# Later batches' squares of q and k: accumulated unfolded by DMA instead of folded on VectorE and then accumulated

## The chip, the cores and the metric

The kernel runs on 1 core of one Trainium2 chip. Its metric is the device time in microseconds (us) of one execution; lower is better. A profile of one execution goes with it, and its times are counted from the start of the profiled span.

## The reference

q, k and v are 4 x 6080 x 256 (batch, rows, columns) in fp32. Cut to what matters:

```
qn = q / (norm(q, over the 6080 rows) + 1e-6)
kn = k / (norm(k, over the 6080 rows) + 1e-6)
a  = softmax(kn^T @ qn / tau)              # 256 x 256 for each batch
x  = (v @ a) as 24320 tokens of 256
h  = relu(x @ w_in)                        # 256 -> 2048
out = (s * h*h + b) @ w_out                # 2048 -> 256
```

The norms are what the change is about: for each batch and each of the 256 columns of q and of k, the sum of 6080 squares.

## The kernel before, in words

**Two kinds of work share the core.** The token part goes through 48 groups of up to 512 tokens, each in 16 steps (`FT`). A step m of group g does the first product (`mm1`, L641: two matmuls into `h_ps`, which has two buffers), seven or eight small matmuls of the second product for the group before (L809), every second step a Relu from PSUM on ScalarE (L651), and squares and sums of the hidden values on VectorE and ScalarE (L662, L664, L735 to L741). VectorE also takes the results out of PSUM (L669). Each group stores 512 KB through the SP queue (L676) and transposes the next v tiles with four DMA transposes on the same queue (L401).

**The attention part runs ahead by one batch.** Batch 0's attention is computed at the start. For b = 1, 2, 3 its pieces are laid between the token steps of batch b - 1 by hand: `at_step(s, f)` puts f after the matmuls of step s, and `po` keeps every engine's instructions in the order in which they are written. A later batch has 12 chunks (`chunks_later`): eleven of 128 partitions with 4 rows each (`JC` = 4), and one of 112. The start step of chunk c is `sc = w0 + span * c * JC / n`; chunks are some 6.75 steps apart in batch 1 and 9.75 in batches 2 and 3. For each chunk:

- `load` (L130): k and q to fp16 by two casting DMAs on the POOL queue, 16 steps ahead of `sc`, into `qk_pool` (8 buffers);
- `mm` (L146): the Gram products of k and q, accumulated in PSUM over the batch;
- `norm_ops`: the squares and what becomes of them, one operation every three steps from `sc` + 3.

**`norm_ops` before the change.** The squares of k (ScalarE, L169) and of q (VectorE, L166) go to a tile `sq` of 128 x 2 x 4 x 256 fp16 in `sq_pool`, which has two buffers for each tag. Two `fold`s on VectorE (L182) add its four rows to two and then to one, giving a tile of 128 x 2 x 1 x 256 (128 KB) in `f3_pool`. Of a later batch, chunk 0's and the last chunk's folded tile are kept in `self.rows`; those of the ten chunks between are added onto chunk 0's by a DMA on the POOL queue (`into_first`, L193):

```
dst, src = self.rows[0][0][0][:np_], st["f", 1][:np_]
po(nc.gpsimd.dma_start(out=dst, in_=src, accum_op=ALU.add))
```

**The end of a batch.** `finish_ops` starts 54 steps ahead of the next batch's first group. Its first operation, `add_norms` (L224), sums the tiles in `self.rows` over the partitions with one-column matmuls; roots, reciprocals, the scaling, the exponentials and the folding of `a` into w_in follow.

**The POOL queue** issues in its written order the loads of k and q, the loads of v (L379, into 4 buffers) and the accumulating DMAs; an instruction that waits holds those behind it.

Of the kernel before, what the change touches and what calls it, by code (L numbers as in the profile page):

```python
# [9 lines left out]
FP16 = mybir.dt.float16  # L10
FP32 = mybir.dt.float32
AF = mybir.ActivationFunctionType
ALU = mybir.AluOpType
# [3 lines left out]
def kernel(  # L17
# [12 lines left out]
    nc = tc.nc  # L30
    P = 128

    B, N, C = q.shape
# [20 lines left out]
    def po(ins):  # L54

        tc.keep_in_program_order(ins)
        return ins

    def pool(name, bufs, **kw):
        return ctx.enter_context(tc.tile_pool(name=name, bufs=bufs, **kw))  # L60
# [3 lines left out]
    wpool = pool("wpool", 1)  # L64
    qk_pool = pool("qk_pool", 8)
    sq_pool = pool("sq_pool", 2)
    f3_pool = pool("f3_pool", 13)
    sm_pool = pool("sm", 1)
    apool = pool("apool", 2)
# [22 lines left out]
    JC = 4  # L92
# [16 lines left out]
    class Gram:  # L109
# [45 lines left out]
        def norm_ops(self, c):  # L155

            qc, kc = self.tiles[c]
            _, np_, jc = self.chunks[c]
            st = {}

            def squares(a, js):
                def f():
                    if "sq" not in st:
                        st["sq"] = sq_pool.tile([P, 2, JC, C], FP16, tag="sq", name="sq")
                    if a == 0:
                        po(nc.vector.tensor_mul(  # L166
                            st["sq"][:np_, 0, js, :], qc[:np_, js, :], qc[:np_, js, :]))
                    else:
                        po(nc.scalar.activation(  # L169
                            out=st["sq"][:np_, 1, js, :], in_=kc[:np_, js, :], func=AF.Square))  # L170
                return f

            def fold(half, arrays, last):
                def f():
                    src = st["f", 2 * half] if 2 * half < jc else st["sq"]
                    if ("f", half) not in st:
                        if last:
                            t = f3_pool.tile([P, 2, 1, C], FP16, tag="f3", name="f3")
                        else:
                            t = sq_pool.tile([P, 2, half, C], FP16, tag=f"f{half}", name="f")  # L180
                        st["f", half] = t
                    po(nc.vector.tensor_add(  # L182
                        st["f", half][:np_, arrays], src[:np_, arrays, :half, :],
                        src[:np_, arrays, half : 2 * half, :]))
                    if last and (self.b == 0 or c == 0 or c == len(self.chunks) - 1):
                        for rows in self.rows:
                            rows.append((st["f", half], np_, 1))
                return f

            def into_first():  # L190

                dst, src = self.rows[0][0][0][:np_], st["f", 1][:np_]
                po(nc.gpsimd.dma_start(out=dst, in_=src, accum_op=ALU.add))  # L193

            def unfolded():
                for rows in self.rows:
                    rows.append((st["sq"], np_, jc))

            ops = []
            for h in range(0, jc, 4):  # L200
                js = slice(h, min(h + 4, jc))
                ops += [squares(1, js), squares(0, js)]
            if jc == 2:
                return ops + [unfolded]
            if jc == 8:
                ops += [fold(4, slice(0, 1), False), fold(4, slice(1, 2), False)]
            ops += [fold(2, slice(0, 2), False), fold(1, slice(0, 2), True)]
            return ops + [into_first] if self.b > 0 and 0 < c < len(self.chunks) - 1 else ops

        def add_norms(self, arrays=(0, 1), last=False):  # L210

# [258 lines left out]
    for c in range(NCH0 - 2):  # L470
        ops = g0.norm_ops(c)
# [11 lines left out]
    ops = [g0.norm_ops(c) for c in (NCH0 - 2, NCH0 - 1)]  # L483
# [21 lines left out]
    acc = opool.tile([P, 4, C], FP32, tag="o_sb", name="acc")  # L505
# [50 lines left out]
    for i, f in enumerate(fin[12:]):  # L556
        at_step(FOLDS[i], f)
    at_step(14, lambda: po(nc.vector.tensor_scalar_mul(
        out=s_out, in0=s_bc, scalar1=1.0 / (LAM * LAM))))
# [341 lines left out]
```

## Time and profile before

| what | us |
|---|---|
| median of 3 runs | 718.86 |
| lowest and highest run | 718.62, 719.0 |
| the profiled execution: its span | 717.2 (717.15 in the trace) |
| runs' median above that span | 1.7 |
| TensorE busy, share of the span | 698.9, 97% |
| VectorE busy | 626.1, 87% |
| ScalarE busy | 536.5, 75% |
| L182 folds, 94 in all, of these 72 for batches 1 to 3 | 0.685 and 0.420 each |
| L193 accumulating DMAs, 30 of 128 KB | 3.1 from issue to landing (median) |

The profiled execution's own time is read from its span, since the page lists no other time for it; the device times of the runs include what lies around the span. "Busy" is the time in which an engine has an instruction at work. PE is TensorE, PEld its weight loads, DVE VectorE, ACT ScalarE, POOL GpSimd, SP SyncE. The DMA share is the mean busy share of the core's 16 DMA engines, in tenths in the page's slices. The granted TensorE clock is 1.000 throughout.

### The profile page before, as it was taken

The page shows a single profiled execution, that of the slowest core. Times are in us where ns is not written, and L with a number is a line of the kernel's source. Part 1 is how long each engine was busy: PE and PEld are TensorE (multiplying, and loading weights), DVE is VectorE, ACT ScalarE, POOL GpSimd, SP SyncE. Part 2 cuts the span into 40 slices and gives each one's busy share as a digit, 9 for nine tenths or more (in the row PEclk, how much of TensorE's full clock was granted, in tenths as well). Part 3 has the DMA queues.
Part 4 walks back from the last instruction along what each step waited for, and adds up shares of the span by engine and source line. Part 5 has one row for each costly group of instructions (what it writes and reads, how often), then busy time and mean ns, then how long its engine had stood idle before and what let it go on. Part 6 is the DMA issues. An engine that isn't in the chain of part 4 may idle for free.

```text
span 717.2 us, 17629 instructions
## 1 busy us (share of the span) xinstructions
PE 698.9 (97%) x7479; PEld 504.6 (70%) x7479; DVE 626.1 (87%) x882; ACT 536.5 (75%) x579; POOL 109.8 (15%) x189
## 2 busy tenths in 40 slices
PE   4799999999999999999999999999999999999998
PEld 2556777776677777777677777777668777777777
DVE  4879999999789999999889899999887888888886
ACT  4479877787777777777777778777877777777875
POOL 4532332101201222111110222110000000000000
PEclk9999999999999999999999999999999999999999
DMA  9999998647556879443972877944423333321201
GB/s 236 207 259 172 159 170 137 111 108 129 119 107 114 144 133 145 108 93 83 154 151 57 141 138 124 154 90 86 105 63 75 93 71 74 97 60 46 83 30 74
DMA packets 89790, 84.25 MB, mean 117 GB/s; under 512 B 59664, under 2 KB 64848, under 8 KB 89712
## 3 DMA queue, kind: packets, MB, share of 16 engines
q0 software_dynamic: 26064, 43.40, 37.5%
q1 hardware_dynamic: 63072, 38.43, 21.5%
q8 instruction: 58, 0.95, 0.6%
q10 hardware_dynamic: 576, 1.31, 0.5%
q14 instruction: 20, 0.16, 0.1%
HBM read 78.91 MB, written 24.90 MB: 145 GB/s over the span
## 4 chain that ended last, share of the span: by engine, by line
PE 93%; DMA 4%; DVE 1%; ACT 1%; POOL 1%; issue 0%; POOLq 0%; ACTq 0%
PE h_ps L641 45%; PE o_ps L809 40%; PE s_ps L146 4%; DMA qk<-in_q_dram 3%; PE wa_ps L326 2%; DMA v<-in_v_dram 1%; PE o_ps L713 1%; PE o_ps L687 0%; POOL qk L130 0%; ACT r L651 0%; DVE o_sb L669 0%; DVE S L737 0%; DVE sq L166 0%; DVE S L735 0%; DVE S L739 0%
## 5 line engine op out<-in xcount | busy, mean ns | idle before, releaser
L651 ACT ACTIVATE r<-h_ps 128x1024 f16<-128x1024 f32 (+1 forms) x384 | 388.4, 1014 | 153.4 <-PE h_ps L641 150.9
L641 PE MATMUL h_ps<-vT,wa 128*128 128x512 f16 (+7 forms) x1632 | 452.1, 364 | 0.1
L809 PEld LDWEIGHTS <-S 128*128 128x128 f16 x2944 | 198.0, 98 | 85.0 <-issue 0.9
L809 PEld LDWEIGHTS <-g 128*128 128x128 f16 x2208 | 155.0, 98 | 74.1
L664 DVE TENSOR_TENSOR g<-r 128x2048 f16<-128x2048 f16 (+2 forms) x150 | 174.8, 1165 | 14.6 <-ACT r L651 14.5
L809 PE MATMUL o_ps<-T,S 128*128 128x128 f16 x2208 | 183.3, 219 | 0.1
L641 PEld LDWEIGHTS <-wa 128*128 128x128 f16 x1632 | 135.9, 98 | 20.6 <-ACT wa L319 0.3
L809 PE MATMUL o_ps<-w_out,g 128*128 128x128 f16 x1472 | 134.2, 219 | 0.2 <-DVE u L669 0.2
L669 DVE SCALAR_TENSOR_TENSOR o_sb<-o_ps,s_out,u 128x256 f32<-128x256 f32 x138 | 66.5, 482 | 47.1 <-PE o_ps L809 44.5
L662 ACT ACTIVATE g<-r 128x1024 f16<-128x1024 f16 (+1 forms) x97 | 100.4, 1035 | 0.2
L146 PE MATMUL s_ps<-qk 128*128 128x256 f16 (+1 forms) x384 | 69.6, 281 | 14.0 <-ACT qk L137 8.7
L379 POOL DMA_DIRECT2D v<-in_v_dram x48 | 31.3, 656 | 263.5 <-DMA vT<-v 209.6
L669 DVE SCALAR_TENSOR_TENSOR u<-o_ps,s_out,rowconst 128x256 f32<-128x256 f32 x138 | 66.0, 478 | 0.0
L809 PE MATMUL o_ps<-w_out,S 128*128 128x128 f16 x736 | 63.5, 219 | 0.0
L809 PE MATMUL o_ps<-N,g 128*128 128x128 f16 x736 | 63.4, 219 | 0.0
L193 POOL DMA_DIRECT2D f<-f x30 | 26.3, 877 | 225.6 <-DVE f L182 172.0
L169 ACT ACTIVATE sq<-qk 128x1024 f16<-128x1024 f16 (+3 forms) x49 | 50.4, 1033 | 10.0 <-DMA qk<-in_k_dram 6.7
L737 DVE TENSOR_TENSOR S<-S,g 128x2048 f16<-128x2048 f16 (+1 forms) x47 | 56.4, 1201 | 1.3
L735 DVE TENSOR_TENSOR S<-g 128x2048 f16<-128x2048 f16 (+1 forms) x47 | 56.1, 1193 | 0.0
L741 DVE TENSOR_TENSOR S<-g,S 128x2048 f16<-128x2048 f16 x46 | 56.0, 1217 | 0.0
L739 DVE TENSOR_TENSOR S<-g 128x2048 f16<-128x2048 f16 x46 | 55.9, 1216 | 0.0
L146 PEld LDWEIGHTS <-qk 128*128 128x128 f16 (+1 forms) x384 | 32.8, 101 | 20.1 <-DVE qk L136 8.0
(74 smaller groups left out, 314.9 us busy)
## 6 DMA issues: line engine op xcount, KB each, us to landing
out_dram<-o_sb SPq DMA_DIRECT2D x46, 512.0 KB, 3.0
v<-in_v_dram POOLq DMA_DIRECT2D x47, 256.0 KB, 4.7
qk<-in_k_dram POOLq DMA_DIRECT2D x42, 256.0 KB, 6.1
qk<-in_q_dram POOLq DMA_DIRECT2D x42, 256.0 KB, 7.2
f<-f POOLq DMA_DIRECT2D x30, 128.0 KB, 3.1
vT<-v SPq DMA_TRANSPOSE x182, 3.2
w<-in_moe_w_out_dram POOLq DMA_DIRECT2D x4, 512.0 KB, 11.3
raw<-in_k_dram SPq DMA_DIRECT2D x2, 512.0 KB, 6.4
```

The source lines that it names most:

```text
L146: po(nc.tensor.matmul(self.s_ps[:, ch, :], kc[:np_, j, ts(ch, P)], qc[:np_, j, :], start=(c == 0 and j == 0 and ch == 0), stop=(c == len(s ...
L169: po(nc.scalar.activation(out=st["sq"][:np_, 1, js, :], in_=kc[:np_, js, :], func=AF.Square))
L641: po(nc.tensor.matmul(dst, wa[:, ci, ts(m, P)], src, start=(ci == 0), stop=(ci == CH - 1), skip_group_check=True))
L651: po(nc.scalar.activation(out=r16[:, :, i % 2, :n], in_=h_tiles.pop((g, i))[:, :, :n], func=AF.Relu))
L662: po(nc.scalar.activation(out=dst, in_=src, func=AF.Square))
L664: po(nc.vector.tensor_mul(dst, src, src))
L669: po(nc.vector.scalar_tensor_tensor(out=dst, in0=src, scalar=s_out, op0=ALU.mult, in1=add, op1=ALU.add))
L735: po(nc.vector.tensor_add(T[1], A21, A22))
L737: po(nc.vector.tensor_sub(T[2], T[1], A11))
L739: po(nc.vector.tensor_sub(T[3], A11, A21))
L741: po(nc.vector.tensor_sub(T[4], A12, T[2]))
L809: po(nc.tensor.matmul(st[name][:, j, :], a()[:, i, ts(j, P)], w[:, i, :], start=first, stop=last, skip_group_check=True))
```

## The change

The ten middle chunks of each later batch are no longer folded. Chunk 0's squares of such a batch go to a tile `sq` of their own in a new pool `acc_pool` with one buffer. Each middle chunk's `sq` tile is added onto it as it is, 128 x 2048 fp16 (512 KB), by an accumulating DMA on the POOL queue, which is now the third operation of a chunk in place of the fifth. After the last chunk's squares come two folds of the accumulated tile and then the two folds of its own. `fold` takes the tile to fold as an argument. Batch 0 is as it was. On VectorE 60 fold instructions fall away; the instructions of TensorE, ScalarE and SP are the same, in the same order; POOL issues as many DMAs as before.

```
+    acc_pool = pool("acc_pool", 1)
...
+            acc = self.b > 0 and c == 0
+
             def squares(a, js):
                 def f():
                     if "sq" not in st:
-                        st["sq"] = sq_pool.tile([P, 2, JC, C], FP16, tag="sq", name="sq")
+                        st["sq"] = (acc_pool if acc else sq_pool).tile([P, 2, JC, C], FP16, tag="sq", name="sq")
...
-            def fold(half, arrays, last):
+            def fold(half, arrays, last, st=st, np_=np_):
...
-                    if last and (self.b == 0 or c == 0 or c == len(self.chunks) - 1):
+                    if last:
                         for rows in self.rows:
                             rows.append((st["f", half], np_, 1))
...
             def into_first():
 
-                dst, src = self.rows[0][0][0][:np_], st["f", 1][:np_]
-                po(nc.gpsimd.dma_start(out=dst, in_=src, accum_op=ALU.add))
+                po(nc.gpsimd.dma_start(out=self.acc["sq"][:np_], in_=st["sq"][:np_],
+                                       accum_op=ALU.add))
...
-            ops += [fold(2, slice(0, 2), False), fold(1, slice(0, 2), True)]
-            return ops + [into_first] if self.b > 0 and 0 < c < len(self.chunks) - 1 else ops
+            if acc:
+                self.acc = st
+                return ops
+            if self.b > 0 and c < len(self.chunks) - 1:
+                return ops + [into_first]
+            if self.b > 0:
+                ops += [fold(half, slice(0, 2), half == 1, self.acc, P) for half in (2, 1)]
+            return ops + [fold(half, slice(0, 2), half == 1) for half in (2, 1)]
```

## The prediction, made before the changed kernel was run

> **What bounds the kernel now.** I read the page's busy table, chain and slices first.
>
> ```profile
> PE 698.9 (97%) x7479; PEld 504.6 (70%) x7479; DVE 626.1 (87%) x882; ACT 536.5 (75%) x579; POOL 109.8 (15%) x189
> ...
> DMA  9999998647556879443972877944423333321201
> ...
> PE 93%; DMA 4%; DVE 1%; ACT 1%; POOL 1%; issue 0%; POOLq 0%; ACTq 0%
> ```
>
> TensorE sets the end: 93% of the chain. So VectorE time taken away is worth only what TensorE waits for VectorE. DMA is full early and light late, so I cut the span into the stretches where batches 1, 2 and 3 are squared.
>
> ```profile
> core 0: us, PE busy (x) PEld busy (x) DVE busy (x) ACT busy (x) POOL busy (x), PEclk, DMA share, GB/s
> ...
> 66.00:78.00 12.00, 11.70 (x123) 8.34 (x121) 11.61 (x16) 12.00 (x18) 2.13 (x4) 1.00 1.14 205
> 78.00:118.00 40.00, 40.00 (x431) 29.53 (x429) 38.12 (x57) 31.16 (x34) 14.29 (x22) 1.00 1.01 159
> 118.00:144.00 26.00, 26.00 (x281) 18.86 (x279) 25.25 (x38) 19.89 (x21) 4.27 (x6) 1.00 0.66 116
> 212.00:300.00 88.00, 87.99 (x949) 64.24 (x946) 80.70 (x114) 67.97 (x71) 18.80 (x29) 1.00 0.71 128
> 385.00:470.00 85.00, 84.99 (x915) 62.16 (x914) 78.89 (x112) 66.14 (x69) 18.72 (x29) 1.00 0.73 129
> ```
>
> TensorE is idle in one of them alone, 66 to 78 us (0.30 us). VectorE is nearly full in batch 1 (38.12 of 40) but holds nobody. The DMA share is the number to keep: 1.01 in batch 1 (over 1 because packets of two queues overlap on an engine), 0.71 and 0.73 in batches 2 and 3. Next, what the edit touches: the folds and their DMA, from the tile view of f, and one such DMA alone on the engines, in slices.
>
> ```profile
> L182 DVE TENSOR_TENSOR f<-sq x47: 680/685/694, 11.6 to 482.4; 128x1024 f16<-128x1024 f16 x44, 112x1024 f16<-112x1024 f16 x3
> L182 DVE TENSOR_TENSOR f<-f x47: 414/420/426, 12.3 to 484.6; 128x512 f16<-128x512 f16 x44, 112x512 f16<-112x512 f16 x3
> ...
> DMA to landing us min/median/max: 2.7/3.1/6.0
> ```
>
> ```profile
> 241.80:242.00 0.20, 0.20 (x5) 0.17 (x4) 0.20 (x1) 0.20 (x1) 0.00 (x0) 1.00 0.73 113
> 242.00:242.20 0.20, 0.20 (x7) 0.20 (x5) 0.06 (x1) 0.01 (x1) 0.13 (x1) 1.00 1.20 179
> 242.20:242.40 0.20, 0.20 (x5) 0.12 (x3) 0.00 (x0) 0.00 (x0) 0.20 (x1) 1.00 1.13 169
> 242.40:242.60 0.20, 0.20 (x2) 0.10 (x1) 0.18 (x1) 0.00 (x0) 0.20 (x1) 1.00 1.09 164
> 242.60:242.80 0.20, 0.20 (x4) 0.15 (x3) 0.20 (x1) 0.00 (x0) 0.20 (x2) 1.00 0.30 31
> ```
>
> The 128 KB accumulate issued at 240.40 moves data from 241.8 to 242.7: about 0.89 us of all 16 engines, at some 170 GB/s, and lands 2.7 us after issue.
>
> **What the Trainium skill says.** All four places are in "DMA: Bandwidth & Descriptors". "Anatomy of one DMA — SWDGE (gpsimd) path" prices a GpSimd DMA at about 2.0 us + bytes/436e3: estimated 2.3 us for 128 KB, 3.2 us for 512 KB. The trace has 2.7 alone and 3.1 median for the first; none shows the second. "SDMA does more than copy" says that the accumulating unit takes at most 2048 elements; a row of the new transfer is exactly 2 x 4 x 256 = 2048, so I count one piece per row; no run shows it yet. "Issuing engines are not separate DMA queues" says that transfers from all issuing engines share 16 DMA engines; the 1.01 and the landing spread of 2.7 to 6.0 agree. "Rules for kernel authors" says that an accumulate reads its destination before it writes it, and that an earlier DMA's semaphore on the same bytes has to be waited for; the program does so, so each accumulate waits for the one before.
>
> **The change part by part.**
>
> *Removed.* Each later batch folded 12 chunks; now it folds the accumulator and its last chunk. 10 chunks x 2 folds x 3 batches = 60 instructions, 30 x (0.685 + 0.420) = 33 us of VectorE. Cover: TensorE, full in every stretch but 66 to 78. There the timeline shows one late u evacuation:
>
> ```profile
> 73.16 0.22 PE L809 MATMUL o_ps<-w_out,g 128*128 128x128 f16 x1 [0.21 <-DVE u L669]
> ```
>
> In those rows the L641 pairs start at 69.80, 71.08, 71.91, 73.49: gaps 1.28 and 1.58, where the next 12 steps take 0.95 on average and at most 1.04. That is about 0.24 + 0.54 = 0.8 us late. Chunk 0's folds of batch 1 stand right there on VectorE (69.57 and 71.69, 1.1 us) and go. ScalarE is full there too, so the gain is 0 to 1.1; I take **-0.8**.
>
> *The transfer grows* from 128 to 512 KB, 30 times. Its engine time: proportional to 0.89 gives 3.5 us (high). It reads two bytes for each that it writes, as the casting fp32 loads do; those run at 208 GB/s written when the engines are full (16 to 36 us), which gives 0.524 MB/208 = 2.5 us (low; 1.2 if only the skill's bytes count). I take 2.8, or +1.9 each, and a landing of 2.7 + 1.9 = 4.6 us alone.
>
> *It moves six steps earlier* (the two folds are no longer ahead of it), to right after the VectorE square; on POOL it is now ahead of one more chunk's k and q loads. Fold of chunk c-1 and square of chunk c were neighbours on VectorE, so accumulate c goes out when accumulate c-1 did, and the loads and v loads behind it keep their times within 1 us; they run four chunks ahead (the load for chunk 6 at 80.1, its squares from 101.7), so none is late. POOL's own issue, 0.88 us, is beside everything.
>
> *The new wait.* sq had two buffers freed by the fold on VectorE. Now the accumulate of chunk c must land before ScalarE can square chunk c+2. Queued behind that square are the Relu evacuations L651, and TensorE waits for those with two h_ps buffers. The room in batch 1 at its tightest (c = 3, the square at 85.47; c+2 = 5):
>
> ```profile
> 85.47 0.69 DVE L166 TENSOR_TENSOR sq<-qk 128x1024 f16<-128x1024 f16 x1
> ...
> 93.09 1.05 ACT L169 ACTIVATE sq<-qk 128x1024 f16<-128x1024 f16 x1
> ```
>
> That is 93.09 - 86.16 = 6.9 us, between 6.9 and 9.5 for c = 1 to 9; in batch 2 the same difference is 12.1 to 15.2. Against a landing of 4.6 alone this holds; what matters is the queue of the DMA engines.
>
> ```profile
> q0 software_dynamic: 3463, 5.50, 78.9%
> q1 hardware_dynamic: 3480, 1.88, 23.5%
> ...
> f<-f POOLq DMA_DIRECT2D x7, 128.0 KB, 4.7
> ```
>
> From 72 to 118 us (seven accumulates, 46 us) shares sum to 102% and the 128 KB transfer already takes 4.7. Seven more times 1.9 = 13.3 us. *Upper bound:* shares add, so 47.1 + 13.3 - 46 = 14 us too much. *Lower bound:* every transfer alone: 14 k and q plus 3 v loads at 0.262/208 = 1.27 (21.6), seven f at 0.89 (6.2), three stores at 1.4 and twelve transposes at 0.33 (8.2, from the late stretch 660 to 700, where three stores and six transposes take 15.4% of 40 us) = 36, + 13.3 = 49.3: 3.3 us too much. The room above a lone landing (2.3 at the tightest) and the h_ps slack (two steps of 0.95 less one Relu of 1.0, about 0.9) absorb some 3 us once. So 0.3 to 11 us. Playing the queue through in order, with the stores and transposes where they stand, I get stalls at chunks 3, 5, 7 and 8 and 2 to 5 us in all; I take **+3.3**. In batches 2 and 3, 0.71 and 0.73 become about 0.9 with room of 12 us: nothing, cover the long chunk interval (9 us against 6.3).
>
> *The end of a batch.* The last chunk's own folds come six steps later, at step +15 and +18 instead of +9 and +12. Batch 1: second fold ended at 142.3; it now stands behind the third S, about 147.5, and the norm matmuls L224 start at 146.8: **+0.6** (0 to 1). In batches 2 and 3 the old folds end at 312.4 and 485.0, the new ones some 6 us later, and L224 starts at 319.6 and 492.2: nothing. The accumulator's fold stands where the last chunk's stood (139.07), 6.9 us after accumulate 10 goes out (132.2); chunk loads are over by then, share 0.66, landing about 5: nothing.
>
> Sum against the profiled execution (span 717.15): -0.8 + 3.3 + 0.6 = **+3.1**, 720.3. The runs' median 718.86 is 1.7 above that span; I carry the 1.7 over: 722.0. A measurement of this kernel can tell about 0.2%, 1.4 us, from no change.
>
> **The rivals.**
> *Hidden* (25%): an accumulate costs 2.5 or less, or q0 and q1 overlap well; every landing stays under 6.9 + 0.9. For it: 40.00 of 40 busy TensorE at a share of 1.01, q0 running dry at 78 to 80 us. Then -0.8 + 0.6 = 718.7.
> *VectorE relief* (10%): the other side. VectorE at 38.12 of 40 makes each evacuation late by queueing; steps there take 0.95, and 0.83 where no Gram product falls in (196 to 201 us). If some 2 us in all of that difference is hidden waiting, not Gram work, it goes: 718.7 - 2 = 716.7. It decides if landing stays hidden and L641 gaps in 78 to 118 us shrink below 0.95; against it, no wait of PE on DVE is listed there.
> *DMA-bound batch 1* (10%): shares truly add and an accumulate costs 3.5: 7 x 2.6 = 18, + 1 for the share already over, - 3 absorbed = 16, - 0.2 for the two small terms: up to 735; half way between that and the main case, 728, is where I start it.
> *Not as said*: the transfer could be cut into smaller pieces per row; it would cost the high 3.5 and falls under the last case.
>
> **How the numbers follow.** Main case 55%, 719.5 to 727, point 722.0. Range 718.0 to 728.0: takes in hidden and the main case with its bounds, leaves out relief and most of the DMA-bound case. Faster 0.10 (relief), same 0.25 (hidden), slower 0.65 (main and DMA-bound).
>
> **What would show it.** The new DMA's landing: about 5 us in batches 2 and 3 and 6 to 10 in batch 1 if I am right, 5 to 7 there if hidden. ScalarE L169 waiting for an accumulate, four or so times between 90 and 126 us; the span between the first and last square of batch 1 grows by 3 us, those of batches 2 and 3 do not. PE idle before L224 in batch 1 about 0.6. L641 gaps around 70 to 73 us shrink to 1.04. I am wrong if batch 2 or 3 grows, or if batch 1 has its old length.

## The result, and the profile after

The changed kernel is **slower by 4.6%**: 753.48 us median of 6 runs (748.95 to 762.27) against 718.98 (718.62 to 719.84); the ratio, which leaves out the slowest of the six because it lies over 1.5% above the fastest, is 1.0464 [1.0428, 1.05]. The forecast was 722.0, in a range of 718.0 to 728.0. The sign was right; the size was short by a factor of ten. The profiled execution took 750.4 us with a span of 748.4, so 31.2 us more than the span of 717.2 before. Every line number below L146 moves a little: the token product `mm1` is now L650, its Relu L660, the second product L818, the square on ScalarE L172, the folds L185, the accumulating DMA L195, the norm matmuls L233.

The page of the changed kernel: the busy times, the DMA share of 40 slices, the chain, and the new DMA's line among the issues (KB each, median us from issue to landing).

```profile
PE 707.2 (94%) x7479; PEld 508.7 (68%) x7479; DVE 602.1 (80%) x822; ACT 537.1 (72%) x579; POOL 110.0 (15%) x189
...
DMA  9999999853944999974594699997333333331201
...
PE 78%; DMA 13%; DVE 3%; ACT 3%; issue 1%; POOL 1%; ACTq 0%; POOLq 0%
...
sq<-sq POOLq DMA_DIRECT2D x30, 512.0 KB, 5.9
```

VectorE lost its 60 folds (882 instructions to 822) and 24.0 us of busy time; instructions that follow one another overlap a little, and summed one by one their durations fell by 33.7 us, the 33 of the prediction. TensorE, with the same 7479 matmuls, is busy 8.3 us longer (707.2 against 698.9) and idle 22.9 us longer (748.4 - 707.2 = 41.2, against 717.2 - 698.9 = 18.3). The two make the 31.2. TensorE's part of the chain fell from 93% to 78%, DMA's rose from 4% to 13%. Who waits for what is in the table of waits: engine, instruction waiting, releaser, us in total, times, the longest.

```profile
ACT sq L172 <- DMA sq<-sq: 26.0, 5, 9.4
...
PE h_ps L650 <- ACT r L660: 21.1, 5, 8.4
```

Five squares on ScalarE wait 26.0 us for an accumulate. Four times TensorE waits for a Relu that stands behind such a square, 20.8 of its 22.9 us of new idling; the fifth wait of its line is 0.27 us at 73.7 us, before the first accumulate moves. This is the wait that the prediction named, at some nine times its size (the stages below grow by 30.0, against the 3.3 forecast). The windows say in which batches (us; each engine's busy time and instructions; granted clock; DMA share; GB/s):

```profile
core 0: us, PE busy (x) PEld busy (x) DVE busy (x) ACT busy (x) POOL busy (x), PEclk, DMA share, GB/s
...
78.00:118.00 40.00, 33.96 (x345) 24.68 (x343) 26.97 (x36) 23.78 (x26) 9.53 (x16) 0.91 1.06 164
118.00:151.00 33.00, 26.61 (x254) 19.03 (x254) 19.53 (x26) 20.31 (x22) 7.63 (x12) 0.90 1.01 164
224.00:312.00 88.00, 81.55 (x885) 59.64 (x883) 68.43 (x88) 59.84 (x62) 15.88 (x25) 0.99 1.00 143
409.00:494.00 85.00, 84.99 (x928) 62.59 (x925) 70.15 (x92) 65.72 (x69) 18.49 (x30) 1.00 0.96 165
```

Batch 1 (first two rows) has lost some 12 us of TensorE time, batch 2 (third row) 6.5, and batch 3 (last row) none, although its DMA share, 0.96, is nearly as high. In 78 to 118 us the share hardly rose (1.01 to 1.06), and the bytes moved per us hardly either (159 to 164 GB/s), with accumulates four times as large to get through. That can be a full queue or packets that stand; the run with plain copies of v below tells the two apart.

The length of a stage, from ScalarE's first to its last square of a batch in the timeline, is the measure of all that follows:

| | batch 1 | batch 2 | batch 3 |
|---|---|---|---|
| before | 70.26 | 97.78 | 97.78 |
| after | 87.66 | 110.38 | 97.67 |
| growth | +17.4 | +12.6 | -0.1 |

With three times about 0.4 us between the stages (72.43, 74.82 and 241.2 us before; 72.97, 75.09 and 241.5 after) and 0.24 us ahead of the first, that is the whole difference of 31.2.

One stall in full. First ScalarE's timeline (start, duration, instruction, and in brackets the idle time before it with its releaser), then TensorE's at the same place.

```profile
88.72 1.02 ACT L660 ACTIVATE r<-h_ps 128x1024 f16<-128x1024 f32 x1
90.53 1.02 ACT L660 ACTIVATE r<-h_ps 128x1024 f16<-128x1024 f32 x1 [0.78 <-PE h_ps L650]
92.39 1.02 ACT L660 ACTIVATE r<-h_ps 128x1024 f16<-128x1024 f32 x1 [0.84 <-PE h_ps L650]
100.15 1.06 ACT L172 ACTIVATE sq<-qk 128x1024 f16<-128x1024 f16 x1 [6.73 <-DMA sq<-sq]
101.11 1.92 ACT L660 ACTIVATE r<-h_ps 128x1024 f16<-128x1024 f32 x2
```

```profile
96.14 0.55 PE L818 MATMUL o_ps<-N,g 128*128 128x128 f16 x7
102.16 1.01 PE L650 MATMUL h_ps<-vT,wa 128*128 128x512 f16 x2 [5.47 <-ACT r L660]
```

The square of chunk 5 wants the `sq` buffer of chunk 3, whose accumulate is still moving. ScalarE stands from 93.4 to 100.15; two Relus stand behind the square; TensorE runs on for 3 us on what it has, and then stands 5.47. What it costs does not end there, as the next windows show (2 us each; the last three columns are clock, DMA share and GB/s):

```profile
96.00:98.00 2.00, 0.69 (x9) 0.45 (x8) 0.06 (x1) 0.00 (x0) 0.00 (x0) 1.00 1.09 156
98.00:100.00 2.00, 0.00 (x0) 0.00 (x0) 0.00 (x0) 0.00 (x0) 0.00 (x0) 0.80 1.31 125
100.00:102.00 2.00, 0.00 (x0) 0.00 (x0) 0.00 (x0) 1.85 (x2) 1.35 (x3) 0.50 0.45 75
102.00:104.00 2.00, 1.84 (x11) 1.22 (x11) 1.85 (x3) 1.03 (x2) 1.16 (x3) 0.50 1.20 198
104.00:106.00 2.00, 2.00 (x12) 1.28 (x11) 1.97 (x3) 0.76 (x1) 0.00 (x0) 0.50 0.92 112
106.00:108.00 2.00, 2.00 (x23) 1.51 (x22) 1.17 (x2) 1.66 (x3) 1.07 (x2) 1.00 1.04 152
```

While TensorE stood, its clock was taken down to 0.50, and it stayed there for its first 4 us of work (12 matmuls in 2 us where 23 are usual). The Trainium skill, "TensorE: Matmul & The Clock Gate", "What's actually happening", has this: after an idle window of some 3.4 us the clock passes at half rate until a busy window has gone by. The trace agrees in kind: at this stall the clock fell 2.5 us after the last matmul and came back 3.8 us after the next one. It stood at 0.50 three times before the end of the kernel:

```profile
99.18:106.01 6.83, 3.85 (x21) 2.51 (x21) 3.83 (x5) 3.65 (x4) 2.50 (x4) 0.50 0.92 127
136.73:143.55 6.82, 5.52 (x31) 3.65 (x31) 2.54 (x4) 4.13 (x5) 2.22 (x3) 0.50 0.69 116
310.81:321.05 10.24, 6.01 (x31) 3.70 (x31) 2.31 (x3) 5.79 (x6) 2.56 (x5) 0.50 1.19 151
```

These hold 15.4 us of matmuls at half rate; at the full clock they would take half of that, so 7.7 of the 8.3 us are here.

**How long an accumulate really takes.** The trace holds a record for each DMA packet. I grouped those of the accumulates (128 packets of 4 KB) and counted the packets of v's transposes (256 bytes) that began between a group's first packet and its last end:

```
accumulate          begin to end     span    transposing packets inside
batch 1, chunk 1      75.0 -  78.2    3.2     168
batch 1, chunk 3      90.7 -  99.7    9.0     680
batch 1, chunk 7     127.8 - 135.6    7.8     540
batch 2, chunk 6     285.0 - 295.4   10.4     573
batch 2, chunk 7     301.1 - 312.7   11.5     975
the other 25                       2.7 - 5.2    0 to 326
```

A packet takes 0.327 us, so 128 on 16 engines are 8 x 0.327 = 2.6 us of engine time. The span leaves out what comes before it: in the four long ones 4.2 to 4.8 us from issue to first packet (1.5 is usual), the queueing that the prediction reckoned with. In the four long ones single packets are recorded with up to 4.84 us: 45 accumulating and 11 transposing packets of this run took over 3 us, none in the kernel before. All four lie in a burst of transposes. A long span takes in more packets for being long, so the count alone proves nothing. But it is the suspicion with which the experiments began: **not the bytes, but the accumulate's meeting with the transposes**. Rivals: the second `sq` buffer is simply too little; 512 KB are simply too much for the queue; the lost folds or the late ones at the batch ends cost it.

### The profile page after: what moved, and what is told of

It reads as the page before. It is cut to its first block, busy times and chain, and to the rows that moved or that the text cites. A ratio compares the mean times of both kernels' runs of the same rounds, so it can differ in the third digit from the quotient of the medians.

```text
span 748.4 us, 17648 instructions
## 1 busy us (share of the span) xinstructions
PE 707.2 (94%) x7479; PEld 508.7 (68%) x7479; DVE 602.1 (80%) x822; ACT 537.1 (72%) x579; POOL 110.0 (15%) x189
## 4 chain that ended last, share of the span: by engine, by line
PE 78%; DMA 13%; DVE 3%; ACT 3%; issue 1%; POOL 1%; ACTq 0%; POOLq 0%
PE h_ps L650 38%; PE o_ps L818 33%; DMA sq<-sq 9%; PE s_ps L147 3%; DMA qk<-in_q_dram 3%; PE wa_ps L335 2%; ACT r L660 2%; DMA v<-in_v_dram 1%; DVE S L744 1%; DVE S L746 1%; PE o_ps L722 1%; ACT g L671 1%; DVE o_sb L678 0%; PE o_ps L696 0%; DVE g L673 0%
## 5 line engine op out<-in xcount | busy, mean ns | idle before, releaser
L660 ACT ACTIVATE r<-h_ps 128x1024 f16<-128x1024 f32 (+1 forms) x384 | 388.0, 1014 | 156.6 <-PE h_ps L650 154.8
L650 PE MATMUL h_ps<-vT,wa 128*128 128x512 f16 (+7 forms) x1632 | 456.1, 367 | 21.2 <-ACT r L660 21.1
L818 PEld LDWEIGHTS <-S 128*128 128x128 f16 x2944 | 199.6, 98 | 87.1 <-issue 3.9
L818 PEld LDWEIGHTS <-g 128*128 128x128 f16 x2208 | 156.3, 98 | 75.4 <-issue 2.4
L818 PE MATMUL o_ps<-T,S 128*128 128x128 f16 x2208 | 184.5, 220 | 0.2
L650 PEld LDWEIGHTS <-wa 128*128 128x128 f16 x1632 | 136.9, 98 | 42.9 <-issue 22.2
L818 PE MATMUL o_ps<-w_out,g 128*128 128x128 f16 x1472 | 135.2, 220 | 0.0
L147 PE MATMUL s_ps<-qk 128*128 128x256 f16 (+1 forms) x384 | 70.4, 284 | 15.4 <-ACT qk L138 8.8
L172 ACT ACTIVATE sq<-qk 128x1024 f16<-128x1024 f16 (+3 forms) x49 | 50.5, 1034 | 35.8 <-DMA sq<-sq 26.0
L818 PE MATMUL o_ps<-w_out,S 128*128 128x128 f16 x736 | 64.4, 221 | 0.0
L818 PE MATMUL o_ps<-N,g 128*128 128x128 f16 x736 | 63.9, 220 | 0.0
L195 POOL DMA_DIRECT2D sq<-sq x30 | 26.4, 881 | 242.6 <-ACT r L660 87.1
```

The source lines that it names most:

```text
L147: po(nc.tensor.matmul(self.s_ps[:, ch, :], kc[:np_, j, ts(ch, P)], qc[:np_, j, :], start=(c == 0 and j == 0 and ch == 0), stop=(c == len(s ...
L172: po(nc.scalar.activation(out=st["sq"][:np_, 1, js, :], in_=kc[:np_, js, :], func=AF.Square))
L650: po(nc.tensor.matmul(dst, wa[:, ci, ts(m, P)], src, start=(ci == 0), stop=(ci == CH - 1), skip_group_check=True))
L660: po(nc.scalar.activation(out=r16[:, :, i % 2, :n], in_=h_tiles.pop((g, i))[:, :, :n], func=AF.Relu))
L818: po(nc.tensor.matmul(st[name][:, j, :], a()[:, i, ts(j, P)], w[:, i, :], start=first, stop=last, skip_group_check=True))
```

## The experiments

### Is it the buffers? Four sq buffers instead of two

```
-  st["sq"] = (acc_pool if acc else sq_pool).tile(...)
+  st["sq"] = (acc_pool if acc else raw_sq_pool).tile(...)    # raw_sq_pool: 4 buffers
```

> The changed kernel with four buffers for the later batches' sq tiles instead of two; nothing else. Theory A (ScalarE's square waits for the accumulate of two chunks before, TensorE for ScalarE): the wait gets two more chunk intervals (12 us and more), which is above the longest landing seen (16.7 us less the old room of 6.9), so the stalls of 6.7, 2.5, 6.7 and 9.4 us go and with them the half-clock stretches after them: 718 to 723 us. Theory B (accumulates in series hold the POOL queue, and with it the loads of k, q and v): the buffers change nothing, 740 us or more.

Measured: 743.07 us (730.69 to 748.77), runs so far apart that no interval was given. The profile with a span of 739.8 has no wait of ScalarE for an accumulate any more, yet the median gains only some 10 of the 34.5 us. Its table of waits:

```profile
PE s_ps L148 <- DMA qk<-in_q_dram: 13.5, 11, 3.9
...
DVE f L186 <- DMA sq<-sq: 8.7, 1, 8.7
```

Batch 1's stage is 71.9, but batch 2's is 107.7: two accumulates took 13.2 and 9.0 us there (590 and 691 transposing packets inside), the loads of k and q behind them were late, and the Gram products waited. They were also issued late, as theory B had it: POOL issued the second of the two at 293.0 us, after the last packet of the first (292.1), and the next loads behind it. At a batch's end the accumulator's fold waited 8.7 us. More buffers move the stall to the next reader; the long transfer is what has to go.

### Is it the bytes, or the adding? A plain copy of the same 512 KB

```
-  po(nc.gpsimd.dma_start(out=self.acc["sq"][:np_], in_=st["sq"][:np_], accum_op=ALU.add))
+  po(nc.gpsimd.dma_start(out=self.acc["sq"][:np_], in_=st["sq"][:np_]))
```

> The changed kernel with a plain copy of the same 512 KB on the same queue in place of the accumulate; the sum over the middle chunks is left out. Theory A1 (what stretches a transfer to 8 to 11 us is an accumulating packet meeting the transposes): a copy reads half the bytes and keeps the engines free, landings under 7 us, 718 to 724 us. Theory C (the bytes alone: engines over-full): half the added bytes remain, landings of 8 us and more beside the transposes stay, 730 us or more.

Measured: 721.69 us (720.06 to 726.69), 1.0044 [1.0027, 1.0061]. The stages are 70.23, 97.67 and 97.67, as before the change. The landing, from the tile view of `sq` (the worst is over the 7 us expected):

```profile
DMA to landing us min/median/max: 2.9/4.2/9.7
```

The longest copy spans 5.3 us, and one met 525 transposing packets in 4.3. In the profiled run (721.14 us) no square waits for a copy. Six of the 16 runs took 724.0 to 726.7 us, with granted clocks down to 0.995, so in some of them something does stand; none of these was traced. And a copy is less work than an accumulate: its packet takes 0.164 us, half of 0.327, so it holds the engines for 1.3 us, and spans of 4.3 and 5.3 are three and four times that. Copies are stretched as well, then, from a shorter start. This alone convicts neither the adding nor the meeting.

### Is it the transposes? Plain copies of v, with and without the change

```
-  po(nc.sync.dma_start_transpose(out=vT[:, :, ts(j, P)], in_=v16[:, j, :]))
+  po(nc.sync.dma_start(out=vT[:, :, ts(j, P)],
+                       in_=v16[:, j, :].rearrange("p (c i) -> p c i", c=CH)))
```

In the changed kernel:

> The changed kernel with each DMA transpose of a v tile replaced by a plain copy of the same 64 KB on the same queue; the transposition of v is left out. Theory A1 (the collision is with the transposes): no accumulate takes over 6 us, no stall, 718 to 724 us. Theory C (bytes alone): the bytes are the same, so stalls stay and the time is 735 us or more.

In the kernel before:

> The kernel before, with the DMA transposes of v replaced by plain copies of the same size (v then stands unturned: the values of x differ, the work doesn't). The baseline that the run of the changed kernel with plain copies (725.86) lacks. If the change alone costs what its stage shows there (4.2 us in batch 1 and about 1.1 at the ends of the batches), this run takes about 725.86 - 5.3 = 720.5 us, 719 to 721.5. If plain copies cost nothing by themselves, 718.9, and some 2 us of the change's cost in that run stand outside batch 1. If it takes 723 or more, the plain copies slow the kernel by themselves and the change costs almost nothing without transposes.

Measured: 725.86 us (724.23 to 726.32), 1.0089 [1.0074, 1.0104], with the change; 719.06 (718.82 to 719.4), 0.9998 [0.9989, 1.0007], without. So plain copies of v cost and save nothing by themselves (the main case of the expectation had laid 1.5 us on them), and **the change costs 6.8 us without the transposes and 34.5 with them**. No accumulating packet takes over 1.2 us any more; the 30 accumulates span 3.0 to 4.8 us. The same shows in small without the change: of the 1 KB accumulating packets of the kernel before, 45 took over 0.5 us, up to 1.65, all in four accumulates with transposes inside; with plain copies of v none took over 0.42. From the table of waits and the tile view of the changed kernel with plain copies:

```profile
ACT sq L172 <- DMA sq<-sq: 5.6, 4, 3.3
```

```profile
DMA to landing us min/median/max: 4.7/5.7/8.8
```

Four waits instead of five, 5.6 us instead of 26.0; batch 1's stage is 74.45, 4.2 longer than before, and batches 2 and 3 are 97.67. (The profiled execution was the lowest of the four, 724.23; with some 0.9 us at the batch ends its stages account for its 5.1 above the other's span of 717.3. The rest of the median's 6.8 isn't in this trace.) That is the stall the prediction reckoned with, in its place and almost in its size, and the landings (8.8 at worst) are those it forecast.

The windows of 78 to 118 us, of the changed kernel and of the kernel before, both with plain copies of v:

```profile
78.00:118.00 40.00, 37.72 (x386) 27.33 (x384) 29.23 (x40) 26.94 (x29) 12.52 (x21) 0.96 1.06 193
...
78.00:118.00 40.00, 40.00 (x431) 29.53 (x429) 38.13 (x56) 31.17 (x34) 14.09 (x22) 1.00 0.92 158
```

At the same share of 1.06 the engines moved 193 GB/s, against 164 with the transposes. So 164 was no ceiling: with the transposes packets were standing. Is it only that plain copies load them less? They are as many packets of the same 256 bytes (49664, median 18 ns in both), but in the kernel before they lower this share from 1.01 to 0.92, some 3.6 us of the 40. If shares add, that is too little for the 13.2 us by which batch 1's stage shortens.

### Buffers again, where the transposes are gone

> Four sq buffers and plain copies in place of the v transposes (the transposition of v is left out). With plain copies alone 725.86 was measured, without any accumulate 720.15. If the 5.7 us between them are ScalarE's wait for a buffer while batch 1's DMA queue is over-full, as the prediction's stall term has it, they go with two more buffers: 719.5 to 722 us. If they are loads that come late or the accumulator's fold waiting, they stay: 724 to 727 us.

Measured (both edits above, four buffers and plain copies): 726.55 us (726.28 to 729.05), 1.0114 [1.0097, 1.0131]. Batch 1's stage is back at 70.23, and nothing is won: from its last square to batch 2's first it takes 79.3 instead of 72.4. The accumulates wait for one another, and what two buffers had paced, four let pile up; batch 1's last accumulate ends at 143.6 us, and the accumulator's fold stands on VectorE before the results that TensorE waits for:

```profile
DVE f L186 <- DMA sq<-sq: 5.3, 1, 5.3
PE o_ps L820 <- DVE o_sb L680: 4.6, 1, 4.6
```

That is the second case of the expectation. I read the 4.2 us of batch 1 as the backlog of a full queue, which no run isolates; a buffer moves where it is paid.

### Smaller pieces

512 KB as 256 rows of 2 KB, and 256 KB after one fold that VectorE does as before:

```
+  wide = (acc_pool if acc else sq_pool).tile([P, 2, JC * C + 32], FP16, ...)   # rows apart, 2 KB each
```

> The changed kernel with a gap of 64 bytes between the q half and the k half of the sq tiles, so that the same 512 KB goes in 256 rows of 2 KB instead of 128 rows of 4 KB. If the length of one accumulating packet (0.33 us here, 0.107 us for the 1 KB of before) is what the transposes get stuck behind, packets of some 0.18 us help: 720 to 735 us. If bytes in flight beside the transposes decide, it stays at 740 to 765 us.

```
-  return ops + [into_first]
+  return ops + [fold(2, slice(0, 2), False), into_first]     # adds 128 x 2 x 2 x 256 onto chunk 0's
```

> The changed kernel with one of the two folds put back on VectorE for every later chunk, so that the accumulate moves 256 KB in rows of 2 KB, half of the change. Theory A1 (an accumulate that meets a burst of DMA transposes is stretched some threefold, and the stall is what goes beyond the room of two buffers): alone some 1.5 us of engine time and a landing of 3.5 us, with transposes 5 to 8, so about at the room of 6.9: 720 to 727 us. Theory D (any accumulate beside transposes hangs for about 8 us, however long it is): stalls as in the changed kernel, 735 us or more.

Measured with rows of 2 KB: 742.31 us (738.98 to 742.79), 1.0316 [1.0293, 1.0339]; batch 1's stage 89.2, the others 97.7. The waits stay:

```profile
ACT sq L174 <- DMA sq<-sq: 20.5, 7, 8.8
...
DVE sq L171 <- DMA sq<-sq: 6.5, 1, 6.5
```

The row's size is not the cause, though it bears on the cost: all four runs lie below the six of the changed kernel (748.95 at the least). That batch 2 came out free here may be the row or the luck of the meeting, and one profile doesn't tell. Measured with 256 KB: 719.87 us (718.98 to 724.77), 1.0014 [1.0006, 1.0022], landing 4.6 median. The profiled run happened to be the 724.77 one: batch 3's stage was 5.3 us longer, with a landing of 13.4 at the worst. So long landings still happen at half the size, but rarely, and the median loses under 1 us. These 128 packets of 2 KB, of some 0.18 us each, come to 1.4 us of the engines, about the plain copy's 1.3, and cost no more than the copy did. So the runs do not tell the adding itself from the time for which it holds the engines.

### The folds: none at all, and where the last ones stand

Without the accumulates (the middle chunks' squares then don't enter the norms), and the same with the accumulator folded at chunk 0's old place:

```
-                return ops + [into_first]
+                return ops
```

> The changed kernel without the accumulating DMAs; the middle chunks' squares are left out of the sums. This is the fold relief alone. My sum of before gives -0.8 + 0.6 = -0.2 us: 718 to 719.5. The rival of VectorE relief gives 716 to 717.5. All theories agree that the 34 us are gone.

> The third term of the prediction's sum. No accumulating DMAs, and chunk 0's tile folded at its old place, so that the last chunk's folds stand at their old steps; the middle chunks' squares are left out of the sums. Without the accumulates but with the late folds 720.15 was measured, 1.1 above before. If the four late folds at the end of each batch are that 1.1: 718.5 to 719.3 us. If it has another cause (the fold relief itself shifts work): 719.8 to 720.5.

Measured: 720.15 us (719.61 to 720.56), 1.0014 [1.0007, 1.0021], without accumulates; 718.83 (718.45 to 720.18), 0.9997 [0.9989, 1.0006], with chunk 0 folded early. The first lies above both of its ranges. Two answers. First, taking the folds off VectorE **gains nothing** that can be told from noise: batch 1's stage is 70.23 in both, against 70.26. The window of 66 to 78 us of the first, where chunk 0's folds are gone too, and TensorE's waits there, before and in that run, say why:

```profile
66.00:78.00 12.00, 11.69 (x122) 8.26 (x120) 10.43 (x13) 12.00 (x18) 5.70 (x11) 1.00 1.13 205
...
PE o_ps L809 <- DVE u L669: 0.2, 1, 0.2
...
PE h_ps L650 <- ACT r L660: 0.3, 1, 0.3
```

The late evacuation by VectorE is gone, and at the same place (73.5 us) TensorE waits for a Relu instead: ScalarE is busy 12.00 of 12 us there as before, and TensorE 11.69 (11.70 before). Second, the late folds at the batch's end cost about 1.3 us (720.15 against 718.83), which show as 0.73, 0.28 and 0.24 us after the three batches. In batch 1, 0.29 of it is the norm matmuls at 147.6 us waiting for the last fold.

### Keeping the two apart by waits

Four `sq` buffers; a tiny copy of the newest vT ahead of each accumulate on POOL, and of the accumulator ahead of the next transposes on SP, so that neither starts before the other has landed:

> The whole computation, four sq buffers, and accumulates kept apart from the v transposes: ahead of each accumulate POOL copies 1 KB of the newest vT tile (so it waits until the transposes have landed), ahead of each group of transposes SP copies 512 B of the accumulator (so it waits until the accumulates have landed). Theory A1 (the collision of the two is what costs): no accumulate spans over 6 us, 719 to 725 us. Theory C (bytes, or the serial chain holding POOL): the added waits make it worse, 735 us or more.

Measured: 795.72 us (792.06 to 796.44), 1.1058 [1.1033, 1.1084]. As a remedy it failed badly; as evidence it fits. No transposing packet falls into an accumulate, and all 30 span 2.8 to 4.7 us, with transposes in the kernel. But its engines are also less crowded: over batch 1's stage, as long as in the changed kernel (87.9 and 87.7 us), the DMA share is 0.84 against 1.05, so this run alone would not tell the meeting from the crowd. What costs is the waiting, in the table of waits:

```profile
POOL look_p L201 <- DMA vT<-v: 168.1, 14, 14.8
...
DVE f L190 <- DMA sq<-sq: 33.8, 3, 20.5
...
PE s_ps L150 <- DMA qk<-in_q_dram: 30.3, 13, 6.7
```

POOL's queue is in order: behind its 14 waits of up to 14.8 us stand the loads of k and q, and TensorE waits for those.

### Making the meeting on purpose, late in the kernel

After 558 us there are only tokens, and DMA is light. I added to the kernel before a 512 KB transfer into a tile of its own in each of twelve groups, beside the transposes: fp32 accumulates from the results (e9), the same meant to go out away from the transposes (e10), plain copies (e11), fp32 accumulates or copies followed by loads of k and q (e13, e15), fp16 accumulates of 128 x 2048 from the hidden tile with and without such loads (e14, e16), and from a tile of their own (e18).

> The disputed cost by itself. The kernel before, and in the late part (groups 34 to 45, no loads of q and k) one extra accumulate of 512 KB for each group, from the group's fp32 result tile to a tile that nobody reads, in rows of 4 KB, released by the same evacuation as the group's store, so that it runs beside the store and the four v transposes. Nothing waits for it. Theory A1 (accumulate and transposes stretch each other): most of these accumulates span 7 us and more where the bytes would take 2.7, and transposes land in 8 us and more. Theory C (shares add): 2.7 + 1.4 for the store + 1.3 for the transposes, so 5.4 us at most. The time itself 718 to 721 us in both.

> As the run before (extra accumulates of 512 KB in the late part, to a tile that nobody reads), but each is issued on POOL behind a load of v, which waits until an older group's transposes have landed, so that it runs without transposes beside it. Both theories: spans of 2.6 to 4 us. If they are long here too, transposes are not the cause. Time 718 to 721 us.

> As the first of these three (beside store and transposes), with plain copies of 512 KB in place of the accumulates. If only accumulating packets collide with transposes, spans of 1.5 to 4 us; if any long transfer from the POOL queue does, 5 us and more, and the accumulate is worse only because it is on the engines longer.

> The kernel before with, in the late part, one accumulate of 512 KB (fp32) for each group beside the transposes and, queued behind it on POOL, two casting loads of 256 KB like those of k and q; all to tiles that nobody reads. Without the loads the accumulates spanned 3.2 to 5.4 us. If accumulate, transposes and queued loads are all three needed for the spans of 8 to 11 us of the changed kernel: several of 7 us or more here. If it is the fp16 form or the timing: 3.2 to 6 us as without loads.

> As the run with loads, but the accumulate is fp16, 128 rows of 2048 elements as in the changed kernel (source: a hidden-value tile; a copy of 1 KB of the result tile ahead of it on POOL gives it the same release). If the fp16 form matters, 7 us or more here and not there; if the loads do, in both.

> As the run with loads, with a plain copy of 512 KB in place of the accumulate. Copies without loads spanned 1.5 to 3.3 us. If the accumulating packets are needed: 2 to 5 us; if any transfer of that size with loads behind it will do: 7 us or more.

> The fp16 accumulate of 128 rows of 2048 beside the transposes, without loads. If the fp16 form alone makes the long spans: 7 us or more; otherwise 3 to 6 us.

> The kernel before with one more 512 KB accumulate of fp16, 128 rows of 2048, in each group from 34 on, from a tile of its own that nothing else uses (its values don't reach the output). It differs from the run that read the hidden tile only in the source. If that run's 98 us came from the hold on the hidden tile, this one takes 719 to 721 us. If an fp16 accumulate beside transposes delays the token steps by itself, it stays above 780. Whether accumulates get stuck: the run before had one of 12 with packets over 3 us; with the meeting as the cause alone one or two of 12 are expected again, with spans of 6 us or more, and the other ten at 3 to 5 us.

| added transfer (one execution each) | us | spans | packets over 3 us |
|---|---|---|---|
| fp32 accumulate | 720.06 | 3.2 to 5.4 | 0 |
| fp32 accumulate, meant to be away | 718.96 | 3.1 to 5.1 | 0 |
| fp32 copy | 720.51 | 1.5 to 3.3 | 0 |
| fp32 accumulate, then loads | 718.98 | 3.9 to 4.5 | 0 |
| fp32 copy, then loads | 720.06 | 2.2 to 3.8 | 0 |
| fp16 accumulate of the hidden tile, then loads | 818.35 | 3.7 to 5.0 | 0 |
| fp16 accumulate of the hidden tile | 817.18 | 3.2 to 6.0 | 11 |
| fp16 accumulate, own tile | 719.01 | 3.1 to 5.0 | 0 |

Mostly a miss. The run "away" was no control: its eight accumulates went out at the same times as in the one beside. And of 68 accumulates, of which 58 met transposing packets (2 to 409 of them), only one got stuck (fp16, 666.2 us, 198 transposing packets inside, packets of up to 3.78 us and only some 10 packets of each kind beginning in a us), without loads of k and q near it. The others span 3 to 5.4 us, and in the two that I followed packet by packet the transposes all but stopped meanwhile (5 to 33 packets a us, against 362 to 443 behind). But plain copies of v do so too beside an accumulate of the changed kernel (down to 11 a us), so that is not what sticks. So the stuck kind can be had without the rest of the changed kernel, but meeting is not enough for it.

The two runs at 817 us are a lesson of another sort. The fp16 source was the tile in which ScalarE writes hidden values:

```profile
DVE g L668 <- ACT r L655: 93.8, 35, 8.9
ACT g L666 <- DMA probe<-g: 78.1, 12, 8.4
...
PE h_ps L645 <- ACT r L655: 63.9, 11, 7.8
```

Twelve times ScalarE waits until the transfer lets go of its tile, 78.1 us in all, and the kernel loses 98; from a tile of their own the same accumulates cost nothing measurable (719.01). The transfers themselves, 3.2 to 6.0 us, are hardly longer than from their own tile; what costs is the hold on a buffer on the way to TensorE, and the granted clock of that run is 0.945.

## Why the prediction was wrong, point by point

- **The bound.** TensorE sets the end and VectorE's work is nearly free: right. Of 33 us of folds taken away, nothing came back that can be told from noise.
- **Fold relief, -0.8 (0 to -1.1):** 0. The end of its bounds at which ScalarE, full in 66 to 78 us, keeps the loss; the wait passed from VectorE to ScalarE.
- **Engine time of an accumulate, 2.8 us:** right: 2.6 by the packets, one for each row of 4 KB as reckoned. Landing alone 4.6: 4.7 to 4.8 at the least, above the 3.2 us that stands in the prediction as an estimate for 512 KB (a plain copy: 2.9 at the least).
- **The path of the stall** (accumulate, `sq` buffer, square on ScalarE, Relu behind it, TensorE): right, and in the waits as written.
- **Its size, +3.3 (0.3 to 11): the step that failed.** It took a landing from shares and durations that add: each transfer keeps its own engine time, whoever is beside it. Where the transposes were gone that was good enough: batch 1 lost 4.2, and landings came to 8.8 at the worst (forecast 6 to 10). But an accumulate that falls into a burst of transposes took 7.8 to 11.5 us instead of 2.6 to 5. The landings of the kernel before, 6.0 at the worst, I had read as queueing. Its packets did show the stretching in small: single accumulating ones of up to 1.65 us instead of 0.109.
- **"In batches 2 and 3: nothing", covered by 12 us of room and the long interval of chunks: wrong for batch 2,** +12.6. The room does not help where one transfer takes 10.4 and the next 11.5 us. Right for batch 3, and for both where the transposes are gone (97.67). A growth of batch 2 or 3 was the sign of being wrong that the prediction had named.
- **The end of a batch, +0.6 in batch 1:** right in place and near in size there (0.73 us by the two runs, of which 0.29 is the wait named), but also 0.28 and 0.24 in the others, where I had put nothing. What costs those, and the rest in batch 1, I did not trace.
- **Not in the sum at all:** the clock after a stall. TensorE's same matmuls took 8.3 us more, 7.7 of them in three stretches at half clock.
- **The rivals.** "DMA-bound batch 1" gave the nearest number, up to 735, by luck, for a cause that the run with plain copies of v refutes: the same accumulates cost batch 1 4.2 us there, not 16. "Hidden" fell with the same run, "relief" with the two on the folds. That the transfer might stretch beyond its share on meeting another kind had no place among them.

What is shown: the large cost needs the transposes (with plain copies of v 27.7 of the 34.5 us are gone, and accumulates kept apart from them are short), and a transfer that holds the engines as long as the 512 KB accumulate does. A plain copy of 512 KB (1.3 us of the engines) and an accumulate of 256 KB (1.4 us) both cost under 3 us in the median. What stays open: whether the adding matters beyond its doubled engine time, what within the DMA engines holds a packet for 3 to 4.8 us, and why some meetings do it and most don't. It is probably also why the changed kernel's runs scatter over 13 us and those of before over 1.2.

## What to carry to other kernels

A sum of DMA shares is no landing time: before an accumulating DMA grows on a queue that also carries DMA transposes, ask when the two meet, and reckon with three to five times its engine time where a buffer hangs on it (7.8 to 13.2 us for 2.6 here). TensorE's stalls of 5.5 us and more cost more than themselves here, because the clock came back late; one of 1.5 us left the clock alone. Taking work off an engine that nobody waits for brings nothing, and another buffer only chooses who waits for a long transfer.

## What the runs showed of the hardware

- A 4 KB accumulating packet within the core took 0.327 us, and a 1 KB one 0.109; 512 KB came to 2.6 us of all 16 engines and landed 4.7 us after issue at best, where a plain copy, with packets of 0.164 us, landed in 2.9.
- An accumulate in a burst of DMA transposes spanned up to 11.5 us (13.2 with four buffers), with single packets up to 4.84; the transposing packets waited too (up to 5.6 us). Beside plain copies of v the longest span was 4.8, the longest packet 1.2.
- After 5.5 us without matmuls TensorE ran at 0.50 of its clock for about 4 us of work.
